# Attention scores of a fused attention and MoE kernel: two row halves, or four quarters, of the matmul array in one step

## The chip, the cores and the metric

One core of one Trainium2 chip runs the whole program. The metric is device microseconds of one execution; the median of several runs is compared. All matmuls of the scores are float32 (each is issued as two weight loads with two products), those of the MoE layers run on pairs of float32r parts (a high and a low part of each operand, three products for one).

## What is computed

The input is q, k, v of 4 batches, 8 heads, 576 tokens, 64 numbers per head. Attention has two parts whose results are added, and two MoE layers follow:

```python
q_d = q.reshape(B, H, Sd, 4, D).mean(axis=3)        # pooled: 144 queries, keys, values
out_d = sm_attn(q_d, k_d, v_d)                      # softmax attention over the pooled tokens
out_up = np.repeat(out_d, 4, axis=2)
mask = np.abs(pos[:, None] - pos[None, :]) < 4      # local: a band of 7 keys for each query
scores = np.where(mask, scale * (q @ k.T), -1e9)
out = out_up + softmax(scores) @ v
x = out as rows of 2304 tokens x 512
x = (sigmoid(x @ w_gate) * (x @ w_val)) @ w_out     # MoE 1, 1536 wide
h = x @ w2_in; y = (h * tanh(softplus(h))) @ w2_out # MoE 2, 2048 wide
```

## The kernel before

**Stages.** Attention of batch 0 comes first (0 to about 78 us of the profile). Then MoE 1 runs batch by batch: `block(b)` emits the products of batch b (`m1`, lines 857 to 859, and `m1out`, lines 888 to 892) and weaves into them the attention of batch b + 1 and the loading, narrowing and splitting of weights. In the profile block 0 lies at about 52 to 232 us (its first products among the last steps of batch 0), block 1 at 232 to 385, block 2 at 385 to 537. Block 3, without attention, and MoE 2 take the rest.

**The scores.** Two heads (parity e = 0 and 1 of a pair) lie above each other on the partitions: e = 0 on 0 to 63, e = 1 on 64 to 127. A score product contracts over 64 numbers, so it uses one half of the array's rows.
- `g_scores(qh, h0)` (line 458) makes pooled scores of half of the queries (72) against 144 keys for two heads of one parity, in one PSUM bank; four such steps make the eight heads. It takes the maxima on VectorE (lines 448, 449) and the exponentials with their sums on ScalarE (line 481), both from PSUM.
- `l_scores(i, e)` (line 567) makes the scores of local tile i for the four heads of one parity: for each head two windows z of 64 queries by 64 keys, whose results lie on partitions 0 to 63 and 64 to 127 of one bank. So one step uses the two column halves of one row half. VectorE adds the mask and copies to SBUF (line 586); the step with e = 1 also takes the maxima, and the one with e = 0 issues the four loads of the next tile's values (`load_vw`, line 340) on SP's queue.

A batch has 10 local steps (5 tiles) and 8 pooled ones (2 halves of the queries).

**PSUM.** Pool `mm` has 5 banks, pool `at` 3. For batches 1 to 3 every attention step takes its banks from `at`; for batch 0 `bank` takes them in turn from both.

**What sets the order.** For batch 0 the list `ORDER[1]` gives the order of the steps by hand. For the other batches `weave` (line 792) keeps a planned clock of TensorE's time: each step has a cost (500 for a pooled step, 660 for a local one, 2952 for a product step of MoE 1) and dependences with a distance on that clock (for batch 1 from the table `ENG`). A step is emitted once its due time is reached and the attention steps are not ahead of their share of the slots. The framework's scheduler then lays the instructions of each engine in order, and may put a later instruction ahead of one that would wait.

Of the kernel before, what the change touches and what calls it, by code (L numbers as in the profile page):

```python
# [8 lines left out]
F32 = mybir.dt.float32  # L9
# [8 lines left out]
# the first batch's loads and steps in the order of their issue  # L18
# [12 lines left out]
# the engines of those steps, and how far apart the second batch's steps are laid (ns)  # L31
# [17 lines left out]
def attn_moe_kernel(  # L49
# [58 lines left out]
    # ---------------------------------------------------------------- memory  # L108
# [21 lines left out]
    # the products of MoE 1 come to lie where the first batch's rows are gone  # L130
# [37 lines left out]
    # ------------------------------------------------- float64 words to float32  # L168
# [24 lines left out]
    # ------------------------------------------------------- weights of MoE 1  # L193
# [15 lines left out]
    def weights(b):  # L209
        """The steps that bring the units of block b on chip and split them."""  # L210
# [76 lines left out]
    # ------------------------------------------------------------- attention  # L287
# [3 lines left out]
    def windows(i):  # L291
        """Of tile i: first query, first key, first row used and rows used, for its halves."""
        q0, n = tiles[i]
        got = []
        for z in range(2):
            want, m = q0 + z * QH, min(QH, n - z * QH)
            first = min(want, S - WK)
            got.append((first, min(max(want - 3, 0), S - WK), want - first, m))
        return got

    def attention(b):
# [43 lines left out]
        # the first batch's rows lie where the products of MoE 1 come later, four neighbouring  # L345
        # tokens of half the sequence to a partition
# [110 lines left out]
        # pooled attention, half the queries at a time; heads in the order (parity, pair)  # L457
        def g_scores(qh, h0):
            def f():
# [6 lines left out]
                ps = bank("ps_g")  # L466
                pv = ps[0:HALF, 0:2 * SD].rearrange("p (h t) -> p h t", h=2)
                e, p0 = divmod(h0, HP)
                for j in range(2):
                    PE.matmul(  # L470
                        pv[:, j, :],
                        lhsT=st.qd[64 * e:64 * e + 64, p0 + j, qh * HALF:(qh + 1) * HALF],
                        rhs=st.kd[64 * e:64 * e + 64, p0 + j, :],
                        start=True, stop=True,
                    )
                sc = scale / (FAC * FAC)
                m, s = st.sm[u]
                neg_max(m[0:HALF, h0:h0 + 2], pv, sc)
                for j in range(2):
                    h = h0 + j  # L480
                    ACT.activation(
                        out=st.E[u][:, h, :], in_=pv[:, j, :], func=AF.Exp, scale=sc,
                        bias=m[0:HALF, h:h + 1], accum_out=s[0:HALF, h:h + 1],
                    )
# [12 lines left out]
        # the same for half of the pairs, with the transposes  # L497
# [68 lines left out]
        # banded attention, two windows of 64 queries by 64 keys at a time  # L566
        def l_scores(i, e):
            def f():
                u = ("l", i)
                if e == 0:  # L570
                    new_stats(u)
                    if b:
                        load_vw(i + 1)
                    st.E[u] = apool.tile([128, HP, 2, WK], F32, tag="El", bufs=3, name="El")
                ps = bank("ps_l")
                pv = ps[:, 0:HP * WK].rearrange("p (h t) -> p h t", h=HP)
                for j in range(HP):
                    for z, (qa, ka, _, _) in enumerate(windows(i)):
                        PE.matmul(
                            pv[64 * z:64 * z + 64, j, :],  # L580
                            lhsT=st.qT[64 * e:64 * e + 64, j, qa:qa + 64],
                            rhs=st.kT[64 * e:64 * e + 64, j, ka:ka + WK],
                            start=True, stop=True,
                        )
                mk = mask[:, 0 if i == 0 else 2 if i == nlt - 1 else 1, :]
                DVE.tensor_tensor(
                    out=st.E[u][:, :, e, :], in0=pv,
                    in1=mk.unsqueeze(1).to_broadcast([128, HP, WK]), op=ALU.add,
                )
                if e == 1:  # L590
# [575 lines left out]
```

## Time and profile before

| | |
|---|---|
| median of 3 runs | 1075.83 us (1075.07 to 1077.99) |
| span of the profiled execution, first to last instruction | 1069.6 us (6.2 below the median) |
| TensorE busy (matmuls) | 1023.1 us, 96% |
| VectorE, ScalarE, GpSimd busy | 690.6, 521.3, 195.2 us |

The device time of a run counts, beside the span, a few microseconds around it; the page gives only the span of its execution. In the rows below PE is TensorE, PEld its weight loads, DVE VectorE, ACT ScalarE, POOL GpSimd, SP the queue engine. Matmuls are pipelined: the duration of one is its latency, and what a stream costs is read from the distance of the starts. A timeline row has the start, the time from the first start to the last end, the engine, line and operation, what is written from what, and the number of instructions.

### The profile page before, as it was taken

The numbers are of one execution on the slowest core, as the hardware profiler recorded it, in microseconds if no ns is written. First come the engines' busy times: TensorE is split into PE (matmuls) and PEld (weight loads), VectorE is DVE, ScalarE is ACT, GpSimd is POOL, SyncE is SP. The second block draws the span as 40 slices with busy tenths as digits, with TensorE's granted clock in tenths as the row PEclk, the third lists the DMA queues.
The fourth block names the chain that finished last, engine by engine and source line by source line (L and its number), as shares of the span: only waits on it lengthen the run. The fifth ranks groups of instructions, "written<-read, shape, count | busy, mean of one in ns | idle before, by whom it ended". The sixth has DMA issues, their size and how long they took to land.

```text
span 1069.6 us, 20453 instructions
## 1 busy us (share of the span) xinstructions
PE 1023.1 (96%) x8152; PEld 956.0 (89%) x8152; DVE 690.6 (65%) x1107; ACT 521.3 (49%) x1222; POOL 195.2 (18%) x235
## 2 busy tenths in 40 slices
PE   4698988999999999999999999999999999999998
PEld 3588978899999999899999999999999999999997
DVE  6977988856975537955488931867555555555552
ACT  4654657346665437565356631654443443433432
POOL 6456564630400400400000002000000000000000
PEclk9998998999999999999999999999999999999999
DMA  8639665777752457622375548212112020220001
GB/s 199 174 103 238 178 204 189 220 241 237 220 184 60 135 179 227 212 101 61 124 243 182 173 167 264 65 29 59 23 37 60 1 60 5 56 60 1 21 1 40
DMA packets 122240, 134.51 MB, mean 126 GB/s; under 512 B 54432, under 2 KB 99488, under 8 KB 122144
## 3 DMA queue, kind: packets, MB, share of 16 engines
q1 hardware_dynamic: 110336, 115.37, 35.1%
q0 software_dynamic: 11808, 17.83, 6.2%
q8 instruction: 64, 1.05, 0.4%
q14 instruction: 32, 0.26, 0.1%
HBM read 101.19 MB, written 31.98 MB: 124 GB/s over the span
## 4 chain that ended last, share of the span: by engine, by line
PE 77%; DVE 11%; DMA 6%; ACT 3%; issue 2%; SPq 0%; POOL 0%; DVEq 0%; ACTq 0%
PE ps_m L857 7%; PE ps_m L859 7%; PE ps_m L858 7%; PE h L1060 6%; PE h L1062 6%; PE h L1061 6%; PE po L1070 6%; PE po L1068 6%; PE po L1069 6%; PE ps_o L888 5%; PE ps_o L890 4%; PE ps_o L892 4%; DVE d L181 2%; DMA raw<-in_moe_w_out_dram 2%; DVE d L185 2%
## 5 line engine op out<-in xcount | busy, mean ns | idle before, releaser
L857 PE MATMUL ps_m<-R 128*128 128x288 f32 (+2 forms) x768 | 236.0, 309 | 4.2 <-DVE sg L863 4.2
L858 PE MATMUL ps_m<-R 128*128 128x288 f32 (+2 forms) x768 | 232.5, 303 | 0.8 <-POOL R L191 0.8
L859 PE MATMUL ps_m<-R 128*128 128x288 f32 (+2 forms) x768 | 232.7, 303 | 0.5 <-POOL R L191 0.5
L857 PEld LDWEIGHTS ps_m<-R 128*128 128x128 f32 x768 | 148.4, 194 | 9.6 <-DVE sg L863 4.6
L190 ACT CAST R<-d 128x512 fp32r<-128x512 f32 (+1 forms) x192 | 108.6, 583 | 89.2 <-PE ps_o L890 34.4
L858 PEld LDWEIGHTS ps_m<-R 128*128 128x128 f32 x768 | 148.8, 194 | 1.9 <-POOL R L191 1.0
L859 PEld LDWEIGHTS ps_m<-R 128*128 128x128 f32 x768 | 148.6, 194 | 1.7 <-POOL R L191 0.9
L191 DVE TENSOR_TENSOR R<-d,R 128x512 fp32r<-128x512 f32 (+1 forms) x158 | 105.5, 682 | 55.1 <-ACT R L190 52.9
L888 PE MATMUL ps_o<-G,R 128*128 128x288 f32 (+2 forms) x384 | 116.5, 303 | 0.0
L890 PE MATMUL ps_o<-G,R 128*128 128x288 f32 (+2 forms) x384 | 114.4, 298 | 0.0
L892 PE MATMUL ps_o<-G,R 128*128 128x288 f32 (+2 forms) x384 | 114.2, 298 | 0.0
L1068 PE MATMUL po<-R,G 128*128 128x512 f32 (+1 forms) x247 | 94.5, 383 | 0.0
L1069 PE MATMUL po<-R,G 128*128 128x512 f32 (+1 forms) x247 | 94.0, 381 | 0.0
L1070 PE MATMUL po<-R,G 128*128 128x512 f32 (+1 forms) x247 | 93.5, 383 | 0.0
L1081 ACT ACTIVATE e<-e 128x1024 f32<-128x1024 f32 (+1 forms) x48 | 40.6, 846 | 107.2 <-DVE e L1080 107.2
L1062 PE MATMUL h<-R 128*128 128x256 f32 x320 | 90.2, 282 | 0.0
L1061 PE MATMUL h<-R 128*128 128x256 f32 x320 | 90.2, 282 | 0.0
L1060 PE MATMUL h<-R 128*128 128x256 f32 x320 | 90.2, 282 | 0.0
L1080 DVE TENSOR_SCALAR e<-h 128x1024 f32<-128x1024 f32 (+1 forms) x48 | 45.9, 956 | 58.3 <-PE h L1062 58.1
L178 ACT ACTIVATE rebias<-raw 128x512 f32<-128x512 f32 x68 | 46.0, 677 | 59.8 <-DMA raw<-in_moe_w_out_dram 23.5
L888 PEld LDWEIGHTS ps_o<-G,R 128*128 128x128 f32 x384 | 72.9, 190 | 1.2
L890 PEld LDWEIGHTS ps_o<-G,R 128*128 128x128 f32 x384 | 73.0, 190 | 0.1
(126 smaller groups left out, 2290.3 us busy)
## 6 DMA issues: line engine op xcount, KB each, us to landing
d<-wd SPq DMA_DIRECT2D x54, 512.0 KB
raw<-in_moe_w_out_dram SPq DMA_DIRECT2D x28, 512.0 KB
wd<-d SPq DMA_DIRECT2D x18, 512.0 KB
wd<-R SPq DMA_DIRECT2D x32, 256.0 KB
raw<-in_moe_w_in_dram SPq DMA_DIRECT2D x16, 512.0 KB
x2d<-R SPq DMA_DIRECT2D x24, 288.0 KB
R<-wd POOLq DMA_DIRECT2D x13, 512.0 KB, 6.9
raw<-in_moe_w_gate_dram SPq DMA_DIRECT2D x12, 512.0 KB
```

What stands on the lines that cost most here:

```text
L857: PE.matmul(p[:, 0:n], lhsT=wh, rhs=xh[:, c, ts], start=(c == 0), stop=False)
L858: PE.matmul(p[:, 0:n], lhsT=wh, rhs=xl[:, c, ts], start=False, stop=False)
L859: PE.matmul(p[:, 0:n], lhsT=wl, rhs=xh[:, c, ts], start=False, stop=(c == KD - 1))
L888: PE.matmul(p[:, 0:n], lhsT=hi[:, o:o + 128], rhs=gt[:, f, 0, ts], start=(f == 0), stop=False)
L890: PE.matmul(p[:, 0:n], lhsT=hi[:, o:o + 128], rhs=gt[:, f, 1, ts], start=False, stop=False)
L892: PE.matmul(p[:, 0:n], lhsT=lo[:, o:o + 128], rhs=gt[:, f, 0, ts], start=False, stop=(f == KF1 - 1))
L1060: PE.matmul(o, lhsT=wi[:, 0, c, cs], rhs=x[:, 0, c, :], start=(c == 0), stop=False)
L1061: PE.matmul(o, lhsT=wi[:, 0, c, cs], rhs=x[:, 1, c, :], start=False, stop=False)
L1062: PE.matmul(o, lhsT=wi[:, 1, c, cs], rhs=x[:, 0, c, :], start=False, stop=(c == KD - 1))
L1068: PE.matmul(p, lhsT=g[:, 0, ts], rhs=w[:, 0, cs], start=(j == 0), stop=False)
L1069: PE.matmul(p, lhsT=g[:, 0, ts], rhs=w[:, 1, cs], start=False, stop=False)
L1070: PE.matmul(p, lhsT=g[:, 1, ts], rhs=w[:, 0, cs], start=False, stop=(j == KF2 - 1))
```

## The change

A pooled step now takes two pairs of heads, both parities, in two banks, and its products alternate between the row halves; there are four such steps in a batch. A local step takes all heads of its tile in two banks and goes around the four quarters of the array; there are five in a batch. Costs in the planner and its names follow. The hand-written order of batch 0 keeps the names `gs.z.0`, `gs.z.2` and `ls.i.1` at their places and loses `gs.z.4`, `gs.z.6` and `ls.i.0`. The rest of the diff takes out comments.

```diff
-        def g_scores(qh, h0):
+        def g_scores(qh, p0):
...
-                ps = bank("ps_g")
-                pv = ps[0:HALF, 0:2 * SD].rearrange("p (h t) -> p h t", h=2)
-                e, p0 = divmod(h0, HP)
+                pvs = [
+                    bank("ps_g")[0:HALF, 0:2 * SD].rearrange("p (h t) -> p h t", h=2) for _ in range(2)
+                ]
                 for j in range(2):
-                    PE.matmul(
-                        pv[:, j, :],
-                        lhsT=st.qd[64 * e:64 * e + 64, p0 + j, qh * HALF:(qh + 1) * HALF],
+                    for e in range(2):
+                        PE.matmul(
+                            pvs[e][:, j, :],
+                            lhsT=st.qd[64 * e:64 * e + 64, p0 + j, qh * HALF:(qh + 1) * HALF],
...
-                neg_max(m[0:HALF, h0:h0 + 2], pv, sc)
+                mv = m[0:HALF].rearrange("p (e h) -> p e h", e=2)[:, :, p0:p0 + 2]
+                for e in range(2):
+                    DVE.tensor_reduce(out=mv[:, e], in_=pvs[e], axis=AX.X, op=ALU.max)
+                DVE.tensor_scalar(out=mv, in0=mv, scalar1=-sc, scalar2=None, op0=ALU.mult)
+                for e in range(2):
+                    for j in range(2):
+                        h = HP * e + p0 + j
+                        ACT.activation(
+                            out=st.E[u][:, h, :], in_=pvs[e][:, j, :], func=AF.Exp, scale=sc,
+                            bias=m[0:HALF, h:h + 1], accum_out=s[0:HALF, h:h + 1],
+                        )
...
-        def l_scores(i, e):
+        def l_scores(i):
...
+                pvs = [
+                    bank("ps_l")[:, 0:HP * WK].rearrange("p (h t) -> p h t", h=HP) for _ in range(2)
+                ]
                 for j in range(HP):
-                    for z, (qa, ka, _, _) in enumerate(windows(i)):
+                    for x in range(2):
+                        for e in range(2):
+                            z = x ^ e
+                            qa, ka, _, _ = windows(i)[z]
...
-            add(("l", "s0", i), l_scores(i, 0), 660.0, deps)
-            add(("l", "s1", i), l_scores(i, 1), 660.0, [(("l", "s0", i), (ENG["L.s1"] if b == 1 else 500.0))])
+            add(("l", "s1", i), l_scores(i), 1000.0, deps)
...
-            for h0 in (0, 4, 2, 6):
-                add(("g", "s", qh, h0), g_scores(qh, h0), 500.0, prev)
-                prev = [(("g", "s", qh, h0), (ENG["L.gs"] if b == 1 else 900.0))]
+            for p0 in (0, 2):
+                add(("g", "s", qh, p0), g_scores(qh, p0), 750.0, prev)
+                prev = [(("g", "s", qh, p0), (2 * ENG["L.gs"] if b == 1 else 1800.0))]
```

The two mask additions of a local step (line 586, one for each bank) and the maxima over all heads stay. The four loads of `load_vw` go with the one step that is left.

## Rows read from the trace of the kernel before

**Rows 1.** The page: busy time of the engines (us, share of the span, instructions).
```profile
PE 1023.1 (96%) x8152; PEld 956.0 (89%) x8152; DVE 690.6 (65%) x1107; ACT 521.3 (49%) x1222; POOL 195.2 (18%) x235
```

**Rows 2.** Stretches (us), busy PE, PEld, DVE, ACT, POOL, then clock, DMA share, GB/s.
```profile
0.00:78.00 78.00, 54.17 (x617) 46.34 (x618) 61.68 (x120) 40.16 (x121) 43.52 (x72) 1.00 0.63 160
78.00:232.00 154.00, 140.00 (x1214) 130.95 (x1213) 127.18 (x191) 84.51 (x249) 95.01 (x94) 0.93 0.71 210
232.00:385.00 153.00, 151.07 (x1391) 144.10 (x1390) 99.45 (x202) 84.33 (x261) 23.48 (x30) 0.99 0.54 169
385.00:537.00 152.00, 148.72 (x1374) 141.47 (x1373) 96.65 (x200) 82.70 (x258) 11.11 (x6) 0.99 0.46 148
```

**Rows 3.** TensorE's longest wait from 232 to 385, and from 385 to 537 us.
```profile
PE ps_m L857 <- DVE sg L863: 1.9, 1, 1.9
...
PE ps_m L857 <- DVE sg L863: 2.2, 1, 2.2
```

**Rows 4.** Chain of waits by line: 232 to 385 us, then 78 to 232.
```profile
by line: PE ps_m L857 17.8%; PE ps_m L859 16.1%; PE ps_m L858 16.1%; PE ps_o L888 9.7%; PE ps_o L890 9.0%; PE ps_o L892 8.9%; PE ps_l L579 3.8%; PE ps_la L664 3.4%; PE ps_g L470 3.3%; PE ps_t L410 2.8%; DVE R L191 2.5%; PE ps_ga L555 1.8%; 
...
by line: DMA raw<-in_moe_w_val_dram 8.5%; DVE d L181 8.4%; DVE d L185 7.8%; DMA raw<-in_moe_w_out_dram 6.8%; issue 5.0%; PE ps_m L859 4.7%; PE ps_m L858 4.6%; PE ps_m L857 4.6%; DVE d L180 4.2%; DMA vw<-in_v_dram 3.4%; PE ps_o L888 2.6%; PE
```

**Rows 5.** The scores' instructions on TensorE, 232 to 385 us, by line.
```profile
L579 PE MATMUL ps_l<-kT,qT 64*64 64x64 f32 x160 | 6.4, 223 | 0.0
L470 PE MATMUL ps_g<-kd,qd 64*72 64x144 f32 x32 | 5.7, 297 | 0.0
```

**Rows 6.** Timeline of TensorE: two local steps together, among the products of MoE 1.
```profile
333.45 0.30 PE L858 MATMUL ps_m<-R 128*128 128x288 f32 x1
333.58 0.29 PE L859 MATMUL ps_m<-R 128*128 128x288 f32 x1
333.80 1.15 PE L579 MATMUL ps_l<-kT,qT 64*64 64x64 f32 x32
...
335.12 0.30 PE L858 MATMUL ps_m<-R 128*128 128x288 f32 x1
...
335.88 1.15 PE L579 MATMUL ps_l<-kT,qT 64*64 64x64 f32 x32
```

**Rows 7.** Timeline of TensorE: one local step by itself.
```profile
258.97 0.68 PE L579 MATMUL ps_l<-kT,qT 64*64 64x64 f32 x16
...
259.82 0.30 PE L858 MATMUL ps_m<-R 128*128 128x288 f32 x1
```

**Rows 8.** Timeline of TensorE: one pooled step by itself.
```profile
300.05 0.29 PE L859 MATMUL ps_m<-R 128*128 128x288 f32 x1
300.27 0.71 PE L470 MATMUL ps_g<-kd,qd 64*72 64x144 f32 x4
...
301.14 0.30 PE L858 MATMUL ps_m<-R 128*128 128x288 f32 x1
```

**Rows 9.** Timeline of TensorE: two pooled steps of different halves, one behind the other.
```profile
118.27 0.72 PE L470 MATMUL ps_g<-kd,qd 64*72 64x144 f32 x8 [0.72 <-DVE qd L441]
```

**Rows 10.** Timeline of TensorE, early: local steps of both halves, and one alone.
```profile
14.16 0.93 PE L579 MATMUL ps_l<-kT,qT 64*64 64x64 f32 x24
...
24.96 1.12 PE L579 MATMUL ps_l<-kT,qT 64*64 64x64 f32 x16 [0.63 <-ACT Eg L481]
```

**Rows 11.** Timeline from a pooled step at 296.25 us: TensorE, VectorE, ScalarE.
```profile
296.25 0.71 PE L470 MATMUL ps_g<-kd,qd 64*72 64x144 f32 x4
...
299.86 0.45 DVE L448 TENSOR_REDUCE m<-ps_g 72x2 f32<-72x288 f32 x1
...
301.44 0.37 ACT L481 ACTIVATE Eg<-ps_g,m 72x144 f32<-72x144 f32 x1
...
301.80 0.37 ACT L481 ACTIVATE Eg<-ps_g,m 72x144 f32<-72x144 f32 x1
```

**Rows 12.** All instructions of line 449: the maxima times a constant.
```profile
L449 DVE TENSOR_SCALAR m<-m x47: 154/164/1255, 23.5 to 520.7; 72x2 f32<-72x2 f32 x32, 128x8 f32<-128x8 f32 x15
```

More of the change, by code (lines that the diff above doesn't have):

```diff
@@ L465, in f @@
                         st.od = apool.tile([128, HP, SD], F32, tag="od", name="od")
-                ps = bank("ps_g")
-                pv = ps[0:HALF, 0:2 * SD].rearrange("p (h t) -> p h t", h=2)
-                e, p0 = divmod(h0, HP)
+                pvs = [
+                    bank("ps_g")[0:HALF, 0:2 * SD].rearrange("p (h t) -> p h t", h=2) for _ in range(2)
+                ]
                 for j in range(2):
-                    PE.matmul(
-                        pv[:, j, :],
-                        lhsT=st.qd[64 * e:64 * e + 64, p0 + j, qh * HALF:(qh + 1) * HALF],
-                        rhs=st.kd[64 * e:64 * e + 64, p0 + j, :],
-                        start=True, stop=True,
-                    )
+                    for e in range(2):
+                        PE.matmul(
+                            pvs[e][:, j, :],
+                            lhsT=st.qd[64 * e:64 * e + 64, p0 + j, qh * HALF:(qh + 1) * HALF],
+                            rhs=st.kd[64 * e:64 * e + 64, p0 + j, :],
+                            start=True, stop=True,
+                        )
                 sc = scale / (FAC * FAC)
                 m, s = st.sm[u]
-                neg_max(m[0:HALF, h0:h0 + 2], pv, sc)
[L479 to L484, printed above, removed]
+                mv = m[0:HALF].rearrange("p (e h) -> p e h", e=2)[:, :, p0:p0 + 2]
[8 more added lines that the diff above has]
+                            bias=m[0:HALF, h:h + 1], accum_out=s[0:HALF, h:h + 1],
+                        )
             return f
@@ L564, in g_av @@
             return f
-        def l_scores(i, e):
+        def l_scores(i):
             def f():
                 u = ("l", i)
[L570 to L576, printed above, removed]
-                for j in range(HP):
-                    for z, (qa, ka, _, _) in enumerate(windows(i)):
[L579 to L584, printed above, removed]
-                mk = mask[:, 0 if i == 0 else 2 if i == nlt - 1 else 1, :]
[L586 to L590, printed above, removed]
-                    E = st.E[u].rearrange("p h e t -> p (h e) t")
-                    if b:
-                        neg_max(st.sm[u][0], E, scale)
-                    else:
-                        DVE.tensor_reduce(out=st.sm[u][0], in_=E, axis=AX.X, op=ALU.max)
@@ new lines, in f @@
+                new_stats(u)
+                if b:
+                    load_vw(i + 1)
+                st.E[u] = apool.tile([128, HP, 2, WK], F32, tag="El", bufs=3, name="El")
+                pvs = [
+                    bank("ps_l")[:, 0:HP * WK].rearrange("p (h t) -> p h t", h=HP) for _ in range(2)
+                ]
+                for j in range(HP):
+                    for x in range(2):
+                        for e in range(2):
+                            z = x ^ e
+                            qa, ka, _, _ = windows(i)[z]
+                            PE.matmul(
+                                pvs[e][64 * z:64 * z + 64, j, :],
+                                lhsT=st.qT[64 * e:64 * e + 64, j, qa:qa + 64],
+                                rhs=st.kT[64 * e:64 * e + 64, j, ka:ka + WK],
+                                start=True, stop=True,
+                            )
@@ new lines, in f @@
+                mk = mask[:, 0 if i == 0 else 2 if i == nlt - 1 else 1, :]
+                for e in range(2):
+                    DVE.tensor_tensor(
+                        out=st.E[u][:, :, e, :], in0=pvs[e],
+                        in1=mk.unsqueeze(1).to_broadcast([128, HP, WK]), op=ALU.add,
+                    )
+                E = st.E[u].rearrange("p h e t -> p (h e) t")
+                if b:
+                    neg_max(st.sm[u][0], E, scale)
+                else:
+                    DVE.tensor_reduce(out=st.sm[u][0], in_=E, axis=AX.X, op=ALU.max)
@@ L705, in attention @@
             for z in range(2):
-                for h0 in range(0, H, 2):
-                    do["gs.%d.%d" % (z, h0)] = (("g", "s", z, h0), g_scores(z, h0), 500.0)
+                for p0 in range(0, HP, 2):
+                    do["gs.%d.%d" % (z, p0)] = (("g", "s", z, p0), g_scores(z, p0), 750.0)
                 for p in range(2):
@@ L712, in attention @@
             for i in range(nlt):
-                for e in range(2):
-                    do["ls.%d.%d" % (i, e)] = (("l", "s%d" % e, i), l_scores(i, e), 660.0)
+                do["ls.%d.1" % i] = (("l", "s1", i), l_scores(i), 1000.0)
                 do["le.%d" % i] = (("l", "e", i), l_exp_all(i), 0.0)
```

4 lines of the change are left out of this document (2 added, 2 removed), and 10 rows, old and new, of the table ORDER.

## The prediction

> **What bounds the kernel now.** The page first: TensorE is busy for 1023 of 1069.6 us, 96% [rows 1], far ahead of VectorE. Busy time of matmuls overstates what they need, so the stretches come next. From 232 to 385 and from 385 to 537 us, where attention of batches 2 and 3 runs between the products of MoE 1, TensorE is busy 151.1 of 153 and 148.7 of 152 us, and VectorE about 99 and 97 [rows 2]. TensorE's longest wait there is 1.9 and 2.2 us, for VectorE, once each [rows 3]. The chain of waits of the first of these goes over TensorE's lines almost throughout, the scores among them with 3.8 and 3.3% [rows 4]. So here TensorE's order of work is the path, and what a score step costs it is paid in full. The stretch from 78 to 232 us (attention of batch 1) is different: 140 of 154 us busy at a granted clock of 0.93, VectorE 127 [rows 2], and the chain names loads of weights and VectorE's narrowing of them ahead of TensorE [rows 4]. Before 78 us TensorE works 54 us and VectorE 62 [rows 2]; there it is a chain through VectorE and loads. After 537 us there are no scores.
>
> **What a score step costs TensorE now.** It is the distance between the products around it, less what these need alone. Products of 288 columns start 0.13 us apart (333.45 to 333.58). With two local steps in between, the last product before and the second one after start 1.54 us apart (333.58 to 335.12) [rows 6]; less two times 0.135, the pair costs 1.27 us. A local step alone has its second product 0.85 us after its start [rows 7], against 1.32 for the pair (333.80 to 335.12) [rows 6]: 0.47 less, so it costs 0.80. The sixteen more starts therefore take 0.029 us each, and some 0.33 us of every interruption has nothing to do with its length: it is going in and coming out. A pooled step alone, with only four starts, costs 1.09 (300.05 to 301.14) less 0.27, 0.82 us [rows 8]. Its four starts lie one behind the other; two pooled steps of different row halves, one behind the other, need 0.72 us for eight starts where the single one needs 0.71 for four [rows 9, 8]. So the halves already work at the same time whenever two such steps meet, and they seldom meet. From 232 to 385 us the 160 starts of local scores are ten steps and the 32 of pooled ones eight [rows 5]; the timeline has six local steps alone and two pairs, and eight pooled ones alone. From 385 to 537 it is the same.
>
> **Part 1, pooled steps.** Eight interruptions of 0.82 become four that look like the meeting pair, 0.83 (0.01 more, 0.72 against 0.71): 6.6 less 3.3, 3.2 us saved for each of batches 2 and 3.
>
> **Part 2, local steps.** Before: six of 0.80 and two pairs of 1.27, 7.3 us. After: five. The unknown is how 32 products go around four quarters. Upper bound: no faster than 32 products of today's pair, 1.27 [rows 6]. Lower bound: the row halves work at once and the step costs what 16 starts cost now, 0.80. The nearest row is an early one, with starts of both halves mixed: 24 took 0.93 us, while 16 of a single half took 1.12 [rows 10]. So all four quarters do work at once there, at 1.8 times the rate; I take 0.80: 5 × 0.80 is 4.0, saved 3.3 us for each batch (at the other end 5 × 1.27, saved 1.0).
>
> A rule of the Trainium skill (TensorE: Matmul & The Clock Gate, "Back-to-back issue gap") speaks against this: it gives a floor of about 25 ns for the distance of two matmuls' starts, however few columns they have. By it 31 distances are 0.78 us in place of 15 × 0.029 = 0.44 now, and a local step would cost 1.14. The rows cannot refuse it: the 0.029 us of the pairs lie above it.
>
> **Blocks 1 and 2 together:** 2 × (3.2 + 3.3) = 13.0 us saved, 8.4 at the other end.
>
> **Part 3, batch 1 (78 to 232 us).** Ten local steps alone, a pooled pair and six pooled ones alone: 8.0 + 5.7 us become 4.0 + 3.3, 6.4 us less of TensorE. Loads and VectorE stand ahead of it in the chain [rows 4], so the bounds are 0 and 6.4; TensorE's lines are a minor part of the chain's head, and I take 2.
>
> **Part 4, batch 0.** Not TensorE's bound. VectorE has four multiplications of maxima fewer, 0.16 us each [rows 12], 0.6 us; but the exponentials of a pooled step now wait for the second reduction, 0.45 us [rows 11], four times, 1.8 us if each is on the chain. I take 0, bounds 2 to either side.
>
> **Part 5, VectorE and SP elsewhere.** Twelve such multiplications fewer, 1.9 us, lie beside TensorE's work in batches 2 and 3 and gain nothing. Mask additions, maxima, exponentials and the four loads of a tile's values are as many as before. The loads come with the merged step, so on SP they move by less than a step's distance; a tile uses them one step later than they are loaded, so I cost that at nothing.
>
> **Part 6, the new wait: banks.** Each step holds two of the three banks. Carrying the planner's rule through with the new costs, I find every score step of batches 2 and 3 by itself among product slots, but one pooled step of the second half directly between the two transposing steps of the first half, and one local step right behind a transposing one. TensorE is in order: a product that waits for a bank holds all products of MoE 1 behind it. Bounds: nothing, if the framework's scheduler puts products there; or, for one place in each of batches 1 to 3, 2.4 us (worked out under the third rival). I take 1 us a batch, 3 in all.
>
> **Sum:** −13.0 − 2 + 0 + 3 = −12 us. The profiled span of 1069.6 would become about 1058; the span lies 6.2 us under the median, which I leave unchanged, so the median goes from 1075.8 to **1064**.
>
> **Rivals.** *First: starts come no closer than the 0.029 us of today, whatever quarter they go to.* Then 32 cost what a pair costs, 1.27. For it: no row shows closer starts at the later pace. Against it: the early row. Then blocks 1 and 2 save 8.4, batch 1 about 1.3 (of 4.1 on TensorE), and 3 are lost: −6.7, **1069**. By the floor of the Trainium skill (same page and section) it would be 0.34 us on each of ten local steps, 1067.
>
> *Second: batch 1 gets all of it.* If TensorE decides after all between 78 and 232 us, and no bank is awaited, it is −13.0 − 6.4, **1056**. For it: 140 of 154 us busy. Against it: the chain.
>
> *Third, the other side: each merged pooled step waits for banks.* Today's step at 296.25 has its maxima taken only 3.6 us later, at 299.86, and its last exponential ends at 302.17 [rows 11]: the bank is held 5.9 us, because VectorE's and ScalarE's queues are full of other work. In the merged step the first bank is held 0.45 us longer, the second more. The next pooled step comes 4.0 us after (300.27, rows 8 and 11) and needs the third bank and the first one: 6.4 − 4.0 = 2.4 us of standstill. Twelve pooled steps of batches 1 to 3 make 28 us, against 15 saved: 1089 at full price. It cancels the gain from 1.25 us a step, and from 1.5 on the kernel is slower; at 1.7 it gives **1081**. Against it: between the two pairs of local steps that the planner lays without anything between them, there are products of MoE 1, at 335.12 and on to 335.88 [rows 6]: where a bank would be awaited the scheduler had placed other work, and in 232 to 537 us no wait for a bank is among the longest.
>
> **How the numbers follow.** A measurement here can tell 0.3%, 3.2 us. Forecast (1058 to 1068): 0.50. First rival: 0.20. Second: 0.10. Bank waits or a slower batch 1 that take back nearly everything, within 3.2 us of today: 0.12. Third: 0.08. Faster is 0.50 + 0.20 + 0.10 = 0.80, the same 0.12, slower 0.08. The range 1055 to 1075 holds the first three but for their tails (0.04) and half of the fourth; 0.18 is left out.
>
> **What would show it.** In 232 to 385 us: four groups of eight pooled starts and five of 32 local ones; a local step's second product following 0.85 us after its first start (1.32 for the first rival); the stretch shorter by 6 us with busy share unchanged. Wrong would be waits of TensorE's score lines for exponentials or mask additions (third rival), a stretch before 232 us that is longer or at a lower clock than 0.93, or groups of 32 that last 1.15 us.

## The result, and the profile after

The changed kernel is slower: 1080.1 us against 1073.4 (medians of 18 runs each), ratio 1.0058 with a 95% interval of 1.0042 to 1.0074. Forecast were 1064 us, 12 less than before; it became 7 more.

The profiled execution of the changed kernel took 1074.5 us with a span of 1072.8, so 1.7 us lie around the span. The span of before, 1069.6, therefore belongs to an execution of about 1071.3 us. The two traces differ by 3.2 us where the medians differ by 6.7; the changed kernel's profiled execution lies 5.6 us under its median, so its trace shows about half of the loss.

The page's line of busy times and the four stretches of the changed kernel (columns as in [rows 2]) answer to [rows 1, 2]:

```profile
PE 1011.3 (94%) x8152; PEld 945.5 (88%) x8152; DVE 686.5 (64%) x1091; ACT 522.3 (49%) x1222; POOL 192.1 (18%) x235
```

```profile
0.00:78.00 78.00, 48.79 (x560) 40.94 (x562) 58.72 (x114) 39.58 (x118) 43.19 (x72) 0.91 0.62 159
78.00:232.00 154.00, 135.91 (x1230) 127.10 (x1226) 123.36 (x190) 84.54 (x249) 92.13 (x93) 0.91 0.68 200
232.00:385.00 153.00, 150.22 (x1419) 144.17 (x1418) 100.58 (x198) 85.86 (x263) 24.85 (x32) 1.00 0.58 178
385.00:537.00 152.00, 145.72 (x1385) 139.19 (x1384) 102.77 (x203) 83.93 (x260) 12.12 (x9) 1.00 0.52 158
```

TensorE is busy 12 us less, as was meant, and the program is longer: the cover went into waits. Before 78 us TensorE works 48.8 us in place of 54.2; the products of MoE 1 come later.

Where the time went is read from the products of MoE 1, whose number did not change. The table has the time from the first product of a block to the first of the next, in us, from one profiled execution of each kernel (the experiments are explained below):

| kernel | first product | block 0 | block 1 | block 2 | block 3 | MoE 2 |
|---|---|---|---|---|---|---|
| before | 51.4 | 191.3 | 150.5 | 151.7 | 114.5 | 406.5 |
| changed | 50.2 | 198.8 | 146.6 | 150.2 | 116.5 | 406.6 |
| merged in batches 2, 3 | 52.0 | 191.2 | 149.1 | 152.3 | 116.8 | 406.6 |
| merged in batch 0 | 49.9 | 207.5 | 148.3 | 153.8 | 114.5 | 406.5 |
| merged in batch 1 | 51.7 | 197.3 | 151.0 | 150.9 | 115.2 | 406.5 |
| merged steps whole, batches 2, 3 | 51.1 | 194.1 | 149.3 | 145.5 | 114.5 | 406.5 |

Block 0, with the last of batch 0 and all of batch 1, lost 7.5 us. Blocks 1 and 2 gained 3.9 and 1.5 where 13 were forecast. A single block of a single execution says little within 2 to 3 us: in the three kernels of this table whose batches 2 and 3 are as before, block 1 takes 148.3 to 151.0 us and block 2 150.9 to 153.8.

Two of the signs that the prediction named for its being wrong are there: the stretches before 232 us have a granted clock of 0.91 (1.00 and 0.93 before), and TensorE's score lines wait for exponentials, as shown below.

**A merged step costs what the sum said.** TensorE's timeline of the changed kernel at a local step, which answers to [rows 7]:

```profile
255.92 0.60 PE L410 MATMUL ps_t<-ident,tok 128*128 128x128 f32 x4
256.45 0.69 PE L593 MATMUL ps_l<-kT,qT 64*64 64x64 f32 x32
257.07 0.40 PE L869 MATMUL ps_m<-R 128*128 128x288 f32 x1
257.31 0.29 PE L870 MATMUL ps_m<-R 128*128 128x288 f32 x1
```

32 products take from first start to last end 0.69 us, as 16 did (0.68). The second product of MoE 1 follows 0.86 us after the step's start; 0.85 were forecast.

**But pooled steps did not stay whole.** All pooled products of block 1 on TensorE (a whole step is x8, one half x4):

```profile
297.92 0.71 PE L474 MATMUL ps_g<-kd,qd 64*72 64x144 f32 x8
...
301.97 0.71 PE L474 MATMUL ps_g<-kd,qd 64*72 64x144 f32 x4
...
307.63 0.71 PE L474 MATMUL ps_g<-kd,qd 64*72 64x144 f32 x4 [2.40 <-ACT Eg L489]
...
316.51 0.71 PE L474 MATMUL ps_g<-kd,qd 64*72 64x144 f32 x4
...
319.87 0.71 PE L474 MATMUL ps_g<-kd,qd 64*72 64x144 f32 x4
...
325.65 0.71 PE L474 MATMUL ps_g<-kd,qd 64*72 64x144 f32 x4
...
328.56 0.71 PE L474 MATMUL ps_g<-kd,qd 64*72 64x144 f32 x4
```

Seven interruptions, where four were forecast and eight stood before. The order of the program has them so: where the framework's scheduler finds one bank free and not two, it lays one half of a step and puts products of MoE 1 ahead of the other. One of the five local steps is torn in the same way (349.5 and 351.5 us).

Why the banks are short is in VectorE's and ScalarE's timelines from the step at 297.92 us on, which answer to [rows 11]:

```profile
303.91 0.81 DVE L484 TENSOR_REDUCE m<-ps_g 72x2 f32<-72x288 f32 x2
...
305.01 0.15 DVE L485 TENSOR_SCALAR m<-m 72x4 f32<-72x4 f32 x1
```

```profile
306.75 0.38 ACT L489 ACTIVATE Eg<-ps_g,m 72x144 f32<-72x144 f32 x1
...
307.12 0.37 ACT L489 ACTIVATE Eg<-ps_g,m 72x144 f32<-72x144 f32 x1
```

The multiplication in the kernel before:

```profile
300.93 0.16 DVE L449 TENSOR_SCALAR m<-m 72x2 f32<-72x2 f32 x1
```

The first bank is free when its second exponential ends, at 307.49: 9.6 us after the step began, where I had 5.9 and 0.45 more. The second reduction has little part in it: the multiplication starts 1.1 us after the first reduction, before (299.86 to 300.93) and after (303.91 to 305.01). VectorE comes to the reductions 6.0 us after the step began, in place of 3.6, and ScalarE to the exponentials 1.7 us after the multiplication, in place of 0.5; both have other work ahead. The half at 307.63 starts 0.14 us after 307.49, having waited 2.4. In block 2 the same wait is 3.0. TensorE's waits from 232 to 385 and from 385 to 537 us, which answer to [rows 3], begin with them:

```profile
PE ps_g L474 <- ACT Eg L489: 2.4, 1, 2.4
PE ps_m L869 <- DVE sg L875: 0.4, 1, 0.4
...
PE ps_g L474 <- ACT Eg L489: 3.0, 1, 3.0
PE ps_m L869 <- DVE sg L875: 2.5, 1, 2.5
```

The Trainium skill has the rule for this (TensorEngine Tiling (Array Packing), "Gotcha 1: PSUM Pressure"): row tiles write to different banks, and row tiling raises the pressure on PSUM. The trace agrees: two banks of three, the first of them held 9.6 us, for 0.7 us of TensorE.

Interruptions of the product stream that contain score products, with their time (distance of the products around, less 0.135 us for one product), worked out from TensorE's timeline:

| kernel | block 1 | block 2 |
|---|---|---|
| before | 16, 17.8 us | 16, 19.1 us |
| changed | 13, 17.2 us | 13, 17.4 us |
| merged in batches 2, 3 | 13, 17.8 us | 13, 16.2 us |
| local steps alone, batches 2, 3 | 13, 15.9 us | 13, 16.8 us |
| merged steps whole, batches 2, 3 | 11, 14.9 us | 11, 13.7 us |

### The profile page after: what moved, and what is told of

It reads as the page before. It is cut to its first block, busy times and chain, and to the rows that moved or that the text cites. A ratio compares the mean times of both kernels' runs of the same rounds, so it can differ in the third digit from the quotient of the medians.

```text
span 1072.8 us, 20416 instructions
## 1 busy us (share of the span) xinstructions
PE 1011.3 (94%) x8152; PEld 945.5 (88%) x8152; DVE 686.5 (64%) x1091; ACT 522.3 (49%) x1222; POOL 192.1 (18%) x235
## 4 chain that ended last, share of the span: by engine, by line
PE 73%; DVE 10%; DMA 7%; ACT 4%; issue 4%; POOL 1%; SPq 0%; ACTq 0%; DVEq 0%; POOLq 0%
PE h L1072 6%; PE h L1074 6%; PE h L1073 6%; PE ps_m L869 6%; PE ps_m L870 6%; PE ps_m L871 6%; PE po L1082 6%; PE po L1080 6%; PE po L1081 6%; PE ps_o L904 4%; PE ps_o L902 4%; PE ps_o L900 4%; DMA raw<-in_moe_w_gate_dram 2%; DVE R L191 2%; DMA x2d<-R 1%
## 5 line engine op out<-in xcount | busy, mean ns | idle before, releaser
L870 PEld LDWEIGHTS ps_m<-R 128*128 128x128 f32 x768 | 148.3, 193 | 4.7 <-POOL R L191 3.5
L191 DVE TENSOR_TENSOR R<-d,R 128x512 fp32r<-128x512 f32 (+1 forms) x158 | 105.8, 680 | 46.6 <-ACT R L190 43.6
L900 PEld LDWEIGHTS ps_o<-G,R 128*128 128x128 f32 x384 | 73.2, 191 | 0.3
L902 PEld LDWEIGHTS ps_o<-G,R 128*128 128x128 f32 x384 | 73.3, 191 | 0.2
L904 PEld LDWEIGHTS ps_o<-G,R 128*128 128x128 f32 x384 | 73.2, 191 | 0.2
```

The lines of the kernel that those rows point to most:

```text
L870: PE.matmul(p[:, 0:n], lhsT=wh, rhs=xl[:, c, ts], start=False, stop=False)
L900: PE.matmul(p[:, 0:n], lhsT=hi[:, o:o + 128], rhs=gt[:, f, 0, ts], start=(f == 0), stop=False)
L902: PE.matmul(p[:, 0:n], lhsT=hi[:, o:o + 128], rhs=gt[:, f, 1, ts], start=False, stop=False)
L904: PE.matmul(p[:, 0:n], lhsT=lo[:, o:o + 128], rhs=gt[:, f, 0, ts], start=False, stop=(f == KF1 - 1))
```

## The experiments

### Which batch loses, and do more banks help

The merged steps are used only in the batches named; the others have the steps, costs and order of before. GS and LS are the batches with merged pooled and merged local steps; `g_scores1` and `l_scores1` are the steps of before.

```diff
+GS, LS = (2, 3), (2, 3)
...
+            if b in LS:
+                add(("l", "s1", i), l_scores(i), 1000.0, deps)
+            else:
+                add(("l", "s0", i), l_scores1(i, 0), 660.0, deps)
...
+            if b in GS:
+                for p0 in (0, 2):
...
+            else:
+                for h0 in (0, 4, 2, 6):
+                    add(("g", "s", qh, h0), g_scores1(qh, h0), 500.0, prev)
```

Both are (2, 3), (0,) or (1,). A fourth kernel has (2, 3) and one bank more for the attention, one less for the products:

```diff
-    mm = tc.alloc_tile_pool(name="mm", bufs=5, space=PSUM, reuse_waits="tile")
-    at = tc.alloc_tile_pool(name="at", bufs=3, space=PSUM, reuse_waits="tile")
+    mm = tc.alloc_tile_pool(name="mm", bufs=4, space=PSUM, reuse_waits="tile")
+    at = tc.alloc_tile_pool(name="at", bufs=4, space=PSUM, reuse_waits="tile")
```

> Merged steps in batches 2 and 3 alone; batches 0 and 1 have the single steps and the order of the kernel before. Theory (the loss lies before 249 us, in the stretch with attention of batches 0 and 1; the gain of the merged steps in batches 2 and 3 is real but cut down by PSUM banks): block 0 lasts 191 us as before, blocks 1 and 2 last 146 to 147 and 149 to 151 us as in the changed kernel, the median is 3 to 6 us under the kernel before (ratio 0.994 to 0.997). Rival (merged steps cost as much as they save wherever they stand, and a slower block 0 is chance): no faster than before, ratio 1.000 or above.

> Merged steps in batch 0 alone. If the loss of block 0 comes from the hand-written order of batch 0, which the merged steps break up, block 0 (first product of MoE 1 of batch 0 to that of batch 1, 191.3 us before, 198.8 after) gets about 6 us longer here and the ratio is about 1.005. If it comes from the steps of batch 1, block 0 stays at 191 and the ratio is 0.998 to 1.001.

> Merged steps in batch 1 alone, which is woven into block 0. If block 0 was lost by the steps of batch 1 (they come at other places between the narrowing of weights, and wait for banks), block 0 gets about 6 us longer and the ratio is about 1.005. If batch 0 did it, block 0 is 191 us or shorter, and the ratio 0.995 to 1.000.

> As the first one (merged steps in batches 2 and 3 alone), with four PSUM banks for attention and four for the products instead of three and five. Theory (with three banks a pooled step of two banks is torn into two single ones and the next one waits 2.5 to 3 us): the pooled steps of each batch stand as eight starts three times out of four, no wait of a pooled step for exponentials is left, blocks 1 and 2 get 2 to 4 us shorter each than in the first one, ratio 0.987 to 0.992. Rival (the products of MoE 1 need their five banks): TensorE's product lines wait for ScalarE and VectorE that empty the banks, and nothing is gained over the first one, or it is slower than before.

| merged in | ratio to before | 95% interval |
|---|---|---|
| batches 2, 3 | 1.0007 | 0.9987 to 1.0027 |
| batch 0 | 1.0100 | 1.0075 to 1.0125 |
| batch 1 | 1.0021 | 0.9995 to 1.0047 |
| batches 2 and 3, with 4 and 4 banks | 1.0035 | 1.0013 to 1.0056 |

Batches 2 and 3 gain nothing: the ratio is the rival's, not the theory's 0.994 to 0.997, though the interruptions there fell by 2.9 us, waits included; where those went is not shown. Batch 0 loses more than the whole change, twice what I had expected, and batch 1 perhaps a little. The three do not add up: together they would lose 1.3%, the whole change loses 0.6%, and its block 0 (198.8 us) is shorter than that of batch 0 alone (207.5) and hardly longer than that of batch 1 alone (197.3). So these runs say what each batch loses by itself, not how the loss of the whole change divides. With a fourth bank blocks 1 and 2 take 145.6 and 148.1 us, 3.5 and 4.2 less than with three, three of four pooled steps stay whole and none waits for exponentials: banks are what tears them. But block 0 (201.7) and block 3 (119.5) pay for the bank that the products lost, and the whole is slower.

### Blocks 1 and 2: the same steps, kept whole

In the first kernel only local steps are merged, in batches 2 and 3 (GS is empty). In the second the pooled steps of the first half of the queries too, planned 6 us apart, and those of the second half single; its edit is shown against the kernel merged in batches 2 and 3. In the program's order of both, every merged step stays whole.

```diff
-            if b in GS:
+            if b in GS and not qh:
...
-                    prev = [(("g", "s", qh, p0), (2 * ENG["L.gs"] if b == 1 else 1800.0))]
+                    prev = [(("g", "s", qh, p0), (2 * ENG["L.gs"] if b == 1 else 6000.0))]
```

> Only the local steps of batches 2 and 3 merged, everything else as before. In the program's order all ten merged local steps stay whole, and the pooled ones are single. Theory A (a merged step is worth what the sum said, and what ate the gain of blocks 1 and 2 was the pooled steps torn for want of banks): 5 interruptions of 0.80 in place of 7.3 us in each of two blocks, 6.6 us in all; ratio 0.993 to 0.996. Theory B (interruptions are not what a step costs; the work comes back as waits elsewhere, whatever is merged): ratio 0.998 to 1.002.

> As the one with local steps alone, and the pooled steps of the first half of the queries merged too in batches 2 and 3, planned 6 us apart (1.8 in the change); those of the second half single, as before. In the program's order every merged step stays whole. Two interruptions by pooled steps fewer in a block, 1.6 us: Theory A: 4.9 us in each block, 9.8 in all, ratio 0.990 to 0.994, and no wait of a pooled step for exponentials over 1 us. Theory B: ratio 0.998 to 1.002, with waits for exponentials as in the changed kernel (2.4 and 3.0 us).

| merged in batches 2, 3 | ratio to before | 95% interval |
|---|---|---|
| local steps | 0.9957 | 0.9935 to 0.9980 |
| local steps, first two pooled ones | 0.9912 | 0.9886 to 0.9938 |

Both ratios lie in the range of Theory A, and the second kernel, 1063.5 us, beats both the kernel before and the changed one. Its pooled steps in block 1, on TensorE:

```profile
297.01 0.71 PE L475 MATMUL ps_g<-kd,qd 64*72 64x144 f32 x8
...
307.41 0.71 PE L475 MATMUL ps_g<-kd,qd 64*72 64x144 f32 x8
...
319.55 0.71 PE L508 MATMUL ps_g<-kd,qd 64*72 64x144 f32 x4
...
325.65 0.71 PE L508 MATMUL ps_g<-kd,qd 64*72 64x144 f32 x4
...
329.02 0.71 PE L508 MATMUL ps_g<-kd,qd 64*72 64x144 f32 x4
```

The two whole steps lie 10.4 us apart, more than the 9.6 for which a bank was held in the changed kernel (9.3 here), and neither waits. Its longest waits in block 1 (245 to 394 us) are not for scores' banks:

```profile
PE ps_gt L578 <- DVE Eg L530: 2.1, 1, 2.1
PE ps_m L947 <- DVE sg L953: 1.8, 1, 1.8
```

Interruptions with scores fall from 36.9 to 28.7 us in the two blocks (the table above), 8.2 less; the runs have 0.88% of 1073, 9.4. The sum had 9.8 for these steps. With local steps alone the interruptions fall by 4.2 us and the runs have 0.43%, 4.6; the sum had 6.6. The length of the two blocks together shows it less well. It is 299.2 to 303.9 us in the seven traces whose batches 2 and 3 are as before, 292.6 to 295.7 in the four with the whole steps (this kernel and three of those below). With local steps alone it is 304.0, in an execution of 1073.05 us, 4.5 above that kernel's median: that trace does not show the gain.

### Does the order around the array matter

The kernel with whole steps, but the products of a step are issued one row half after the other, in pooled and in local steps.

```diff
-                for j in range(2):
-                    for e in range(2):
+                for e in range(2):
+                    for j in range(2):
...
-                for j in range(HP):
-                    for x in range(2):
-                        for e in range(2):
-                            z = x ^ e
+                for e in range(2):
+                    for j in range(HP):
+                        for z in range(2):
```

> As the one with all merged steps of batches 2 and 3 whole (ratio 0.9912), but the products of a merged step are issued half by half: all of one row half, then all of the other, instead of alternating. If the array needs alternation, a local step alone has its 32 starts in 0.9 to 1.0 us (16 x 0.029 twice) in place of 0.48, and costs 1.27 in place of 0.80: 0.47 us on ten steps, 4.7 us, ratio 0.995 to 0.996. If steps overlap as soon as they stand behind each other, starts in 0.48 to 0.6 us and a ratio of 0.990 to 0.993.

The ratio is 0.9917 (0.9887 to 0.9948), the same as going around within what the runs can tell. A local step, going around (first) and half by half (second), one row from TensorE's timeline of each kernel:

```profile
366.21 0.69 PE L623 MATMUL ps_l<-kT,qT 64*64 64x64 f32 x32
```

```profile
363.35 0.98 PE L622 MATMUL ps_l<-kT,qT 64*64 64x64 f32 x32
```

Half by half a step takes 0.29 us more (first to last start 0.76 us in place of 0.48), between the two cases of the expectation. Four of the ten steps of the kernel that goes around (at 336.9, 338.8, 482.8 and 484.7 us) had been laid half by half by the scheduler anyway, so 6 × 0.29 = 1.7 us are left. The interruptions of the two blocks are 1.8 us longer (30.5); the runs cannot tell so little.

### Batch 0: a queue, or the steps themselves

In the changed kernel the first 96 products of MoE 1 take 40.9 us, 32.5 before. The chain of waits from 60 to 93 us goes over GpSimd, which adds up values of batch 1 (vd, L426 and L428), waits for their loads, and only then makes the last split of batch 0's rows (R, L191), for which TensorE's products wait:

```profile
78.25 1.66 POOL vd L428 x4
79.91 0.45 POOL R L191
80.35 3.02 DMA araw<-in_v_dram
83.44 0.52 POOL vd L426
83.97 0.41 POOL vd L428
84.38 1.13 POOL R L191
85.55 0.66 PE ps_m L870
```

After the wait the products run at the lower of the two levels, 1.2 GHz. Stretches around it, columns as in [rows 2]; 80.5 to 85.5 is the wait:

```profile
80.50:85.50 5.00, 1.80 (x14) 1.44 (x11) 4.72 (x6) 2.30 (x5) 3.17 (x6) 0.89 0.48 119
85.50:91.20 5.70, 5.65 (x20) 5.66 (x21) 1.41 (x2) 0.98 (x2) 2.42 (x4) 0.50 1.02 202
91.20:95.00 3.80, 3.80 (x25) 3.80 (x25) 0.78 (x2) 2.12 (x4) 3.80 (x6) 1.00 1.13 289
```

So the first theory was GpSimd's order. The edit queues batch 1's adds behind the last split, in the changed kernel and, as a control, in the kernel before.

```diff
+                with ExitStack() as behind:
+                    if b == 1:
+                        behind.enter_context(tc.issue_after(splits[3]))
                     eng.tensor_tensor(out=o, in0=raw[:, :, 0, :], in1=raw[:, :, 1, :], op=ALU.add)
```

> The changed kernel with one thing more: GpSimd's pooling of batch 1's values (the adds of vd from araw) is queued behind the last split of batch 0's rows that GpSimd makes (R from xn). In the changed kernel's trace the first 96 products of MoE 1 take 40.9 us against 32.5 before, and the two late splits stand behind 12 and 15 adds of vd, some of which wait for loads (79.87 and 84.34 us; before behind 6 and 9 adds, 75.43 and 79.60). Theory A (the order on GpSimd's queue is what batch 0 lost by): the splits come at about 75 and 77 us, the first 96 products take 34 to 37 us, the time falls by 4 to 6 us, ratio to the kernel before 1.000 to 1.002. Theory B (the merged steps' own chain over VectorE and ScalarE, or TensorE's clock, is the cause): the products behind the splits wait for something else, the first 96 take 39 us or more, ratio 1.004 to 1.006.

> The kernel before with the same edit, as a control. Both theories: here the splits stand behind 6 and 9 adds, and only the second has waited for one load (1.1 us), so it can gain 0 to 3 us by itself, ratio 0.997 to 1.000. What it gains here is to be taken off what the edit gains in the changed kernel.

The changed kernel stays at 1.0066 (1.0041 to 1.0091); the control goes to 1.0051 (1.0027 to 1.0076). Theory A falls as it was put. The first 96 products take 36.5 us, within the range of Theory A, but the next 192 take 45.7 in place of 39.0; that batch 1's values come later would explain it. The 39 us of Theory B were not reached either. The control loses too, where I had given it a gain of up to 3 us; its profiled execution is its quickest (1073.85 us, median 1079.47) and does not show where. So the edit costs something by itself, and putting GpSimd in order does not bring the time back.

### Batch 0: which of the two steps, and what in it

Pooled steps alone, local steps alone, and both with one more edit: maxima and multiplication for each half by itself, as before the change.

```diff
-                for e in range(2):
-                    DVE.tensor_reduce(out=mv[:, e], in_=pvs[e], axis=AX.X, op=ALU.max)
-                DVE.tensor_scalar(out=mv, in0=mv, scalar1=-sc, scalar2=None, op0=ALU.mult)
                 for e in range(2):
+                    neg_max(mv[:, e], pvs[e], sc)
                     for j in range(2):
```

> Only the pooled steps of batch 0 merged (batch 0 with both kinds merged gave 1.010, first 96 products 43.2 us against 32.5). In the changed trace the exponentials of batch 0's pooled steps start 1.5 us later (25.55 against 24.08 us), because they wait for the maxima of both halves, and GpSimd's norms and splits follow. Theory A (the pooled steps are the cause): ratio 1.006 to 1.010, first 96 products 38 us or more. Theory B (the local steps, which hold two of the eight banks, are the cause): ratio 0.999 to 1.003, first 96 products 32 to 35 us.

> Only the local steps of batch 0 merged. Theory A: ratio 0.999 to 1.003, first 96 products 32 to 35 us. Theory B: ratio 1.005 to 1.010, first 96 products 38 us or more. If both this and the one with pooled steps alone cost about half, neither is the cause by itself.

> Both kinds merged in batch 0 alone, as in the run that gave 1.010, but the pooled step takes maxima and multiplication for each half by itself, as the kernel before did, so that the exponentials of the first half wait for the first reduction alone. Theory A (the late exponentials are what batch 0 lost by): ratio back to 1.000 to 1.004, the exponentials of the first pooled step at about 24 us. Theory B (banks and the order of the steps): ratio 1.008 to 1.011 as without it.

| merged in batch 0 | ratio to before | 95% interval | first 96 products |
|---|---|---|---|
| both kinds | 1.0100 | 1.0075 to 1.0125 | 43.2 us |
| pooled steps | 1.0080 | 1.0048 to 1.0112 | 43.5 us |
| local steps | 0.9976 | 0.9957 to 0.9996 | 33.2 us |
| both, maxima by half | 1.0003 | 0.9979 to 1.0028 | 32.4 us |

The pooled steps are the cause, as Theory A had it (the local ones even gain a little), and in them the one multiplication for both halves: the last kernel differs from the first by this alone. The first 96 products are a rough measure: in kernels whose batch 0 is as before they take 32.5 to 38.1 us (38.1 in the kernel with whole steps), in the three with this multiplication and no edit of GpSimd's order 40.9 to 43.5. The first exponential of batch 0 in the kernel before, with both kinds merged, and with maxima by half (ScalarE's timelines):

```profile
24.08 0.38 ACT L481 ACTIVATE Eg<-ps_g,m 72x144 f32<-72x144 f32 x1 [9.96 <-DVE m L449]
```

```profile
25.55 0.38 ACT L490 ACTIVATE Eg<-ps_g,m 72x144 f32<-72x144 f32 x1 [10.74 <-DVE m L486]
```

```profile
24.80 0.38 ACT L488 ACTIVATE Eg<-ps_g,m 72x144 f32<-72x144 f32 x1 [10.35 <-DVE m L450]
```

Half of the delay came back there, not all as I expected (24.80 in place of about 24 us), and all of the time did. Further on, the last pooled products of batch 0 start at 58.94 us before, at 62.90 with both merged and at 58.85 with maxima by half; the first of these on TensorE, and the second:

```profile
58.94 0.71 PE L470 MATMUL ps_g<-kd,qd 64*72 64x144 f32 x4 [0.36 <-ACT Eg L481]
```

```profile
62.90 0.71 PE L475 MATMUL ps_g<-kd,qd 64*72 64x144 f32 x4
```

In the order of the program 57 products of MoE 1 stand ahead of the second row and 27 ahead of the first and of the kernel with maxima by half. So the delay is laid into the order of the program, as where steps of batches 2 and 3 were torn. The local steps behind follow, and the last split with them (86.30 us with both merged, 79.60 before, 79.64 with maxima by half). How much of this is the longer hold of the banks itself, and how much the order laid because of it, no run parts.

### The change with both repairs

Maxima by half in all batches of the changed kernel; the best kernel with batch 0's local steps merged; that with batch 1's local steps too; and the change without batch 1 with both repairs.

```diff
-GS, LS = (2, 3), (2, 3)
+GS, LS = (2, 3), (0, 2, 3)
...
+GS, LS = (2, 3), (0, 1, 2, 3)
...
+GS, LS = (0, 2, 3), (0, 2, 3)
```

The first kernel has the edit shown above and no other. The rest start from the kernel with whole steps; the last of them has the maxima by half as well, in all its merged pooled steps.

> The changed kernel with one edit: in every merged pooled step the maxima and the multiplication are taken for each half by itself, so that the exponentials of the first half, and its bank, wait for the first reduction alone. Alone in batch 0 this edit moved the ratio from 1.010 to 1.000. Theory A (the change lost in batch 0 by the late exponentials, and elsewhere only what banks tore): block 0 back to 190 to 194 us (198.8 in the changed kernel), ratio 0.994 to 0.999. Theory B (batch 1's merged steps, or both batches together, cost by themselves): block 0 at 196 us or more, ratio 1.000 to 1.004.

> The best so far (0.9912: merged steps of batches 2 and 3 kept whole) with the local steps of batch 0 merged too (alone 0.9976). If the two gains add up: 0.987 to 0.991. If what block 0 gains is lost again in its later part, as with the edit on GpSimd's queue: 0.990 to 0.994.

> As the one before, and the local steps of batch 1 merged too. If batch 1's stretch follows VectorE and loads, as the prediction had it, this adds nothing: ratio as the one before within 0.002. If the merged steps of batch 1 cost by themselves (merged with the pooled ones alone: 1.002): 0.002 to 0.005 higher. If TensorE decides there: 0.002 to 0.004 lower.

> The change without batch 1, with both repairs: maxima for each half by itself, and in batches 2 and 3 the pooled steps of the first half planned 6 us apart and those of the second half single. Theory A: the gain of the whole merged steps (8.8 per mille) and nothing lost in batch 0: ratio 0.989 to 0.993. If the merged pooled steps of batch 0 still hold their banks too long: 0.995 to 1.000.

| kernel | ratio to before | 95% interval |
|---|---|---|
| changed, maxima by half | 1.0028 | 1.0008 to 1.0048 |
| whole in 2, 3, local in 0 | 0.9918 | 0.9895 to 0.9941 |
| whole in 2, 3, local in 0, 1 | 0.9913 | 0.9883 to 0.9943 |
| whole in 2, 3, both in 0, maxima by half | 0.9941 | 0.9920 to 0.9962 |

The early maxima alone take about half of the loss away. The ratio and block 0, 197.6 us, lie in the ranges of Theory B: batch 1's merged steps, or both batches together, cost by themselves. The first 96 products are back at 33.0 us, but products 288 to 576 (those of lines `m1` and `m1out` together), among the attention of batch 1, take 73.0 (70.0 in the changed kernel, 67.9 before). With both kinds merged in batch 1 they take 69.2 to 73.0 in four traces, in all others 62.4 to 67.9. There a merged local step is torn, 8 products and 24, and the second part waits for its bank, which VectorE's mask additions hold; TensorE and VectorE in this kernel:

```profile
194.12 0.45 PE L591 MATMUL ps_l<-kT,qT 64*64 64x64 f32 x8
...
201.51 1.12 PE L591 MATMUL ps_l<-kT,qT 64*64 64x64 f32 x24 [6.94 <-DVE El L599]
```

```profile
201.05 0.74 DVE L599 TENSOR_TENSOR El<-ps_l,mask 128x256 f32<-128x256 f32 x2
```

In the changed kernel the same wait is 2.8 us (at 199.57), with batch 1 alone merged 3.5 (at 195.76); the kernel before has 0.3 us at most (at 160.52). From 78 to 232 us VectorE of the changed kernel is busy 123 of 154 us, and an addition that comes late keeps two banks. That batch 1 with merged steps of both kinds loses by this is what the waits suggest; the runs of batch 1 alone leave it within what they can tell, and with local steps alone merged it costs nothing (0.9913 against 0.9918). As I expected, batch 1's local steps change the ratio by less than 0.002.

Neither kernel with merged steps in batch 0 improves on the 0.9912 of the best. Batch 0's local steps gained 0.24% alone; on top of the whole steps the ratio falls into the range of a gain lost again (0.990 to 0.994), but its interval holds parts of both ranges. With both kinds and both repairs it is 0.9941, between the two forecasts: not as good as hoped, and not all lost.

## Why the prediction was wrong, step by step

**What bounds the kernel.** Right for blocks 1 and 2: fewer interruptions there shorten the program by nearly what they cost, 9.4 us measured for 9.8 summed, once the steps stay whole (with local steps alone 4.6 for 6.6).

**Parts 1 and 2, the price of a step.** Right. 0.86 us to the second product against 0.85; a pooled step of eight starts 0.71 [rows 8, 9]. The **first rival** falls with it. So does the rule that I had weighed (the Trainium skill, TensorE: Matmul & The Clock Gate, "Back-to-back issue gap"): 32 starts in 0.48 us are 0.0155 us apart, under its floor of 25 ns. The trace of the kernel before could have refused it: in the pair of local steps at 333.80 us the two column halves start 6 to 8 ns apart; the 0.029 us was a mean. Another section of the same page bears on the case and I had passed over it: "The mechanism" (of packing small matmuls) says that products of different tiles of the array start about 4 ns apart. The trace has 5 to 8 ns within a round of the four quarters, and 58 ns from round to round (106 from the first to the second).

**Part 1, the number of interruptions.** This step failed: "eight interruptions become four". They became seven, because a merged step asks for two banks of three at once. I had asked only how long a step would wait for banks (Part 6), not whether it would stay whole; the planned distance of 1.8 us in the change against the 6.4 that I had for the hold would have told it.

**Part 6, banks.** The mechanism was seen and sized too small. I took 1 us a batch; measured were waits of 2.4 and 3.0 in blocks 1 and 2, and the tearing, which no part had. I had 6.4 us for the hold of the first bank, from a single step's 5.9 [rows 11]; it was 9.6, and not by the second reduction, on which I had put the whole difference: VectorE came to the reductions 2.4 us later than in that row, and ScalarE to the exponentials 1.2 us later after the multiplication. Parts 1, 2 and 6 together were to give 11 us in blocks 1 and 2 (13.0 less 2 of the 3); the kernel merged in these batches alone gave none.

**Part 4, batch 0.** The largest miss, and the other step that failed: 0 with bounds of 2, measured 1.0% with batch 0 merged alone, 10.6 us between the medians. I had counted the exponentials' wait as 0.45 us each, four times, and nothing behind them. The pooled steps alone lose 0.8%; with both kinds merged in batch 0 the early maxima give all of the 1.0% back, and in the whole change about half of its loss.

**Part 3, batch 1.** Forecast −2 with bounds of −6.4 and 0; the run with batch 1 alone has 1.0021, 2.2 us slower, its interval across one. A loss was not in the bounds. The reason against a gain, VectorE ahead of TensorE, may also be the reason for a loss, since VectorE holds the banks; the waits suggest it and no run settles it.

**Part 5** was not tried by itself.

**The rivals.** The second (batch 1 gets all of it) falls. The third had the right side and the right mechanism, banks held until exponentials are done, and even the 2.4 us, by luck: it came from a hold of 6.4 and a distance of 4.0, where the hold was 9.6. Not each pooled step waited: the scheduler tore the steps and let one wait in each block, and the rival left out batch 0, which loses 1.0% by itself. It had a chance of 0.08.

## What to carry to other kernels

Joining small matmuls that use different parts of the array is worth what it saves in interruptions, and no more than the accumulator banks allow: before merging, compare how long a bank is held until its last reader is done with how far apart the merged steps come, here 9.6 us against 1.8, and spread the steps or merge fewer of them. Do not let the first half's readers wait for the second half's reduction: one multiplication for two halves in place of two cost 1.0% (1.0100 against 1.0003) in the batch where the readers were on the path. And when a queue shows up in the chain of waits, test it with a control in the old kernel before naming it the cause.

## What the runs showed of the hardware

- Four quarters of the array (64 rows by 64 columns, float32) take a product each within 20 ns, and each round of four starts 58 ns after the one before (106 ns between the first two); half by half the same 32 products take 0.98 us in place of 0.69.
- A wait of TensorE was paid twice: after 5 us with little work (80.5 to 85.5 us, TensorE busy 1.8) the granted clock was 0.50 for 5.7 us, and 1.00 after that.
